# Dilated gated convolution on one core: load order, weight sums and first tiles by piece, last tiles transposed on TensorE, output-projection passes merged

## The chip, the cores and the metric

The kernel runs on one core of one Trainium2 chip. TensorE does the matrix products and transposes, VectorE and ScalarE the elementwise work, GpSimd some setup; a DMA is a copy between memories, issued from the queue of ScalarE, GpSimd or SyncE (SP). A semaphore is a counter that a finished step raises and a waiting one reads. The metric is the device time of one execution in microseconds (us). Before the change it is 387.62 us, the median of the three runs made before the prediction (386.77 to 388.38). Each run has its mean granted TensorE clock, as a share of full speed (0.971 in the profiled run of before).

## The reference, cut to what matters

```python
B, T, D, K = 2, 16000, 144, 15          # x: (B,T,D)  w: (K,D,2D)  w_o: (D,D), all bf16
dil = 2; pad = (K - 1) * dil            # 28
xp = pad x at the front by 28
h = sum over i of  xp[:, pad - 2*i : pad - 2*i + T, :] @ w[i]      # (B,T,288)
f, g = h[..., :144], h[..., 144:]
out = (tanh(f) * sigmoid(g)) @ w_o
```

The sequence is cut into 128 stretches of 250 steps, one per partition. A "tile" is one step of all 128 stretches, and an "oct" is 8 tiles. The 144 input channels are split into 128 (buffers with an A) and 16 (with a B, eight steps packed into one 128-row tile). The kernel saves multiplications: it works with sums of weights (WC, WS, WB[2]) and differences of tiles (VE, VF, DU, DE, DF, BE, BF). So VectorE has to prepare weight sums and tile differences before TensorE can begin its steady loop.

## The kernel before: the parts that matter

The kernel records operations with what they read and write. A list scheduler then fixes an order for each engine, and semaphores are planned from that order. The order is fixed when the program is built, so an instruction that waits holds everything behind it on its engine (in the trace of after, two weight loads on ScalarE's queue stand 4.72 us, and ScalarE's first copy comes behind them).

```python
# weights: three pieces on ScalarE's queue, three completion semaphores ("wa": 3 at the end)
wa_pieces = [(0, 5), (5, 10), (10, 15)]
for pi, (t0, t1) in enumerate(wa_pieces):
    g.add("act", ld_w(t0, t1), w=[("WA", pi)], dma="wa", ...)
...                                     # then the two WB loads, also on ScalarE's queue
# ScalarE: copies of the first x tiles (XBc, XA), then halving of the gate half of each piece
    g.add("act", lambda a: a.activation(WA[:, a_:b_, D:N2], ..., scale=0.5), w=[("WA", pi)])
# x: chunks of 32 steps in a ring of three, all queued at once on the other queue (SP)
XCH = 32
# weight sums: whole-array sums, after all pieces
wsum(WC[:, 1], WA[0,4,8,12], WA[2,6,10,14]);  wsum(WC[:, 2, 0:3], ...);  wsum(WC[:, 0], ...)
wsum(WS[:, 0:7], WA[even], WA[odd])
# out-projection weights, scaled by 0.5 on GpSimd
g.add("pool", lambda p: p.tensor_scalar(WOR[:], WOR[:], 0.5, None, ALU.mult), ...)

# a completion semaphore is taken from a small pool; a DMA that takes one again
# first waits for the DMA that had it before
def assign(self, mksem, dma_sems):
    ...
            slot = pool.pop(0); pool.append(slot)
            if slot[2] is not None:
                op.deps.add(slot[2])
    ...
g.assign(mksem, {"xp": 8, "wa": 3, "wb": 2, "xr": NX, "xa": 4, ...})

# out-projection of one oct: DMA transpose of Z, then two matmuls of 144 columns per tile
def ship(o):
    g.add("sp", lambda e: e.dma_start_transpose(ZT[...], Z[...]), dma="zt", ...)
    for dl in range(a, c):
        for part in range(2):
            t.matmul(PS[:, cc:cc + D], lhsT=ZT[:, zt, dl + part, :], rhs=WOR[:, 2*dl + part, :])
    ...                                 # ScalarE copy to OS, store
```

Cut: the tile differences, the four-stage loop S1 to S4 over 62 half-octs, tanh and gate (`finish_pair`), and the launch.

## Time and profile before

| | before |
|---|---|
| median time, us | 387.62 |
| span of the profiled run, us | 385.4 |
| mean granted TensorE clock in it | 0.971 |
| TensorE without a gap from / to, us | 36.45 / 375.7 |
| last weight piece lands, us | 22.33 |
| start of the last convolution matmul to the end (the tail), us | 10.01 |

The first view is the strip of 40 equal slices on the page of before: a digit is the busy share in tenths, and PEclk is the granted clock.

```profile
PE   5156999999999999999999999999999999999992
PEclk9559999999999999999999999999999999999997
```

TensorE is full from the fifth slice to the last but one. What can be gained lies at both ends.

The second view is the chain of waits of before, at the head: start, duration, what it was.

```profile
2.75 19.58 DMA WA<-in_w_dram
...
22.35 0.81 ACT WA L441
...
23.19 5.93 DVE WC L450 x2
...
29.14 0.62 DVE WC L450
...
36.02 0.38 DVE DD L646
...
36.45 2.87 PE PS L553 x22
```

The weights land at 22.33 us. Two sums then take 5.93 us together, while the next sum takes 0.62. The reason shows in GpSimd's timeline of before: its scaling of the out-projection weights ran at the same time.

```profile
22.37 6.04 POOL L724 TENSOR_SCALAR WOR<-WOR 128x2304 bf16<-128x2304 bf16 x1 [6.29 <-DMA WOR<-in_w_o_dram]
```

The third view is the same chain at the tail, after the last convolution matmul.

```profile
375.75 0.66 ACT TS L582
...
376.43 0.47 DVE Z L586
...
376.92 3.23 DMA ZT<-Z
...
380.20 2.20 PE PS L610 x16
```

The DMA transpose costs 3.23 us, and the sixteen matmuls behind it run at 0.138 us each; the same matmuls take 0.0625 us in the loop. The granted clock is 1.00 in the loop, 0.76 from 379 to 381 us and 0.50 after that.

### The profile page before, as it was taken

The numbers are of one execution on the slowest core, as the hardware profiler recorded it, in microseconds if no ns is written. First come the engines' busy times: TensorE is split into PE (matmuls) and PEld (weight loads), VectorE is DVE, ScalarE is ACT, GpSimd is POOL, SyncE is SP. The second block draws the span as 40 slices with busy tenths as digits, with TensorE's granted clock in tenths as the row PEclk, the third lists the DMA queues.
The fourth block names the chain that finished last, engine by engine and source line by source line (L and its number), as shares of the span: only waits on it lengthen the run. The fifth ranks groups of instructions, "written<-read, shape, count | busy, mean of one in ns | idle before, by whom it ended". The sixth has DMA issues, their size and how long they took to land.

```text
span 385.4 us, 7697 instructions
## 1 busy us (share of the span) xinstructions
PE 358.0 (93%) x3154; PEld 290.6 (75%) x3154; DVE 244.7 (63%) x629; ACT 173.1 (45%) x355; POOL 21.0 (5%) x31
## 2 busy tenths in 40 slices
PE   5156999999999999999999999999999999999992
PEld 5035888888888888888888888888888888888871
DVE  1759998766666757766666677666666665544340
ACT  2312453545445544454455444544544445444442
POOL 8660000000000000000000000000000000000000
PEclk9559999999999999999999999999999999999997
DMA  8972979785547457565437444654356433211222
GB/s 229 381 146 45 248 139 243 148 220 118 101 111 212 78 116 112 124 180 118 88 92 115 90 101 101 117 115 88 91 116 87 101 78 90 64 40 54 63 51 72
DMA packets 111599, 47.03 MB, mean 122 GB/s; under 512 B 103678, under 2 KB 106159, under 8 KB 110669
## 3 DMA queue, kind: packets, MB, share of 16 engines
q1 hardware_dynamic: 108826, 44.96, 52.7%
q10 hardware_dynamic: 2227, 1.25, 1.3%
q8 instruction: 24, 0.39, 0.4%
q0 software_dynamic: 512, 0.33, 0.3%
q14 instruction: 10, 0.08, 0.1%
HBM read 11.82 MB, written 9.22 MB: 55 GB/s over the span
## 4 chain that ended last, share of the span: by engine, by line
PE 89%; DMA 6%; DVE 3%; ACT 1%; ACTq 0%; issue 0%
PE PS L553 80%; PE PS L610 8%; DMA WA<-in_w_dram 5%; DVE WC L450 2%; DMA ZT<-Z 1%; DVE WS L450 0%; ACTq L342 0%; DVE Z L586 0%; ACT WA L441 0%; DVE STA L470 0%; DVE DU L499 0%; DVE VE L499 0%; DVE VF L499 0%; ACT TS L582 0%; ACTq L334 0%
## 5 line engine op out<-in xcount | busy, mean ns | idle before, releaser
L582 ACT ACTIVATE TS<-PS 128x576 bf16<-128x576 f32 x125 | 81.3, 650 | 100.8 <-PE PS L553 100.4
L586 DVE SCALAR_TENSOR_TENSOR Z<-TS 128x288 bf16<-128x288 bf16 x125 | 56.8, 455 | 42.3 <-ACT TS L582 42.0
L553 PE MATMUL PS<-WA,DE 128*128 128x288 bf16 x496 | 81.0, 286 | 0.0
L553 PE MATMUL PS<-WS,DU 128*128 128x288 bf16 x434 | 71.0, 286 | 2.1 <-DVE DD L646 2.1
L553 PE MATMUL PS<-WA,DF 128*128 128x288 bf16 x434 | 71.0, 286 | 0.0
L643 ACT ACTIVATE U<-PS 128x288 f32<-128x288 f32 x62 | 25.4, 410 | 71.1 <-PE PS L553 71.0
L553 PEld LDWEIGHTS PS<-WA,DE 128*128 128x128 bf16 x496 | 47.8, 98 | 11.2
L553 PEld LDWEIGHTS PS<-WS,DU 128*128 128x128 bf16 x434 | 42.3, 98 | 12.9 <-DVE DD L646 2.4
L615 ACT ACTIVATE OS<-PS 128x432 bf16<-128x432 f32 (+1 forms) x94 | 42.7, 487 | 20.4 <-PE PS L610 20.4
L553 PEld LDWEIGHTS PS<-WA,DF 128*128 128x128 bf16 x434 | 42.2, 98 | 10.3
L646 DVE TENSOR_TENSOR DD<-PS,U 128x288 f32<-128x288 f32 x62 | 28.3, 457 | 30.2 <-PE PS L553 19.7
L610 PE MATMUL PS<-WOR,ZT 128*128 128x144 bf16 x500 | 42.4, 229 | 4.5 <-DMA ZT<-Z 4.5
L610 PEld LDWEIGHTS PS<-WOR,ZT 128*128 128x128 bf16 x500 | 35.9, 99 | 8.4 <-DMA ZT<-Z 4.8
L553 PE MATMUL PS<-WC,VE 128*128 128x288 bf16 x248 | 40.5, 286 | 0.9 <-DVE VE L499 0.9
L553 PE MATMUL PS<-WC,XA 128*128 128x288 bf16 x248 | 40.5, 286 | 0.0
L499 DVE TENSOR_TENSOR BF<-XB 128x512 bf16<-128x512 bf16 x31 | 13.1, 423 | 37.5 <-PE PS L553 37.5
L553 PE MATMUL PS<-WB,XB 128*128 128x288 bf16 x128 | 36.6, 289 | 0.0
L553 PE MATMUL PS<-WB,BE 128*128 128x288 bf16 x124 | 35.5, 286 | 0.0
L553 PE MATMUL PS<-WB,BF 128*128 128x288 bf16 x124 | 35.5, 286 | 0.0
L553 PE MATMUL PS<-WC,VF 128*128 128x288 bf16 x186 | 32.9, 286 | 0.0
L660 DVE TENSOR_TENSOR PS<-PS,DD 128x288 f32<-128x288 f32 x62 | 28.6, 462 | 5.6 <-PE PS L553 0.9
L657 DVE TENSOR_TENSOR PS<-PS,DD 128x288 f32<-128x288 f32 x62 | 28.7, 462 | 0.8 <-PE PS L553 0.7
(61 smaller groups left out, 350.8 us busy)
## 6 DMA issues: line engine op xcount, KB each, us to landing
out_dram<-OS SPq DMA_DIRECT2D x31, 288.0 KB, 2.1
Xr<-in_x_dram SPq DMA_DIRECT2D x7, 1152.0 KB, 6.6
WA<-in_w_dram ACTq DMA_DIRECT2D x3, 360.0 KB, 14.3
Xr<-in_x_dram SPq DMA_DIRECT2D x1, 864.0 KB, 4.5
ZT<-Z SPq DMA_TRANSPOSE x32, 3.3
Xp<-in_x_dram SPq DMA_DIRECT2D x2, 252.0 KB, 5.5
XA<-STA SPq DMA_TRANSPOSE x31, 3.2
XB<-STB SPq DMA_TRANSPOSE x31, 3.2
```

The source lines that it names most:

```text
L450: g.add(eng, lambda v: v.tensor_tensor(dst(), a(), b(), ALU.add), r=r, w=wk, dur=dur)
L499: return g.add("dve", lambda v: v.tensor_tensor(dst(), a(), b(), ALU.subtract), r=r, w=wk, dur=dur)
L553: return lambda t: t.matmul(bank(b), lhsT=lhs(), rhs=rhs(), start=start, stop=True, skip_group_check=True)
L582: return a.activation(TS[:, s, :, :], src, ACT.Tanh)
L586: return v.scalar_tensor_tensor(dst, TS[:, s, :, D:N2], 1.0, TS[:, s, :, 0:D], ALU.add, ALU.mult)
L610: return t.matmul(PS[:, cc_:cc_ + D], lhsT=ZT[:, zt, dl_ + part_, :], rhs=WOR[:, 2 * dl_ + part_, :], start=first, stop=True, skip_group_c ...
L615: return a_.activation(OS[:, os_, a0:c0, :].rearrange("p e d -> p (e d)"), PS[:, bo * 512:bo * 512 + (c0 - a0) * D], ACT.Copy)
L643: g.add("act", lambda e: e.activation(U[:, u, :], bank(a), ACT.Copy), r=[("bank", a)], w=[("U", u)], dur=0.43)
L646: g.add("dve", lambda v: v.tensor_tensor(DD[:, u, :], bank(b), U[:, u, :], ALU.subtract), r=[("bank", b), ("U", u)], w=[("DD", u)], dur=0.48)
L657: g.add("dve", lambda v: v.tensor_tensor(bank(c), bank(a), DD[:, u, :], ALU.add), r=[("bank", a), ("DD", u)], w=[("bank", c)], dur=0.48)
L660: g.add("dve", lambda v: v.tensor_tensor(bank(e), bank(b), DD[:, u, :], ALU.subtract), r=[("bank", b), ("DD", u)], w=[("bank", e)], dur=0.48)
```

## The change

The intent:

1. Queue the x chunks, all but the first 8 steps, behind the last weight piece. Make the first chunks smaller (8, 8, 16, then 32).
2. Cut the weights into four pieces, and form weight sums and the first two ("direct") tiles piece by piece.
3. Delete the scaling on GpSimd. The factor 0.5 goes into an existing ScalarE copy.
4. Merge neighbouring out-projection matmuls that share a transposed block: 11 instead of 16 per oct, with the same columns in all.
5. In the last oct, transpose Z on TensorE instead of by DMA, two tiles at a time.

```diff
-        wa_pieces = [(0, 5), (5, 10), (10, 15)]
+        wa_pieces = [(0, 4), (4, 8), (8, 12), (12, 15)]
...
+    CH = [(0, 8), (8, 16), (16, 32)] + [(c, min(c + XCH, 8 * NOCT)) for c in range(32, 8 * NOCT, XCH)]
+        load_xchunk(1).deps.add(wa_op)            # likewise for all later chunks
...
-        g.add("pool", lambda p: p.tensor_scalar(WOR[:], WOR[:], 0.5, None, ALU.mult), ...)
+                    return a_.activation(OS..., PS..., ACT.Copy, scale=0.5)
...
-        wsum(lambda: WC[:, 1, :, :], lambda: wev(0, 4), lambda: wev(2, 4), wak, [("WC", 1)], 0.7)
+        for i in range(4):                        # sums of piece i as soon as it is there
+                wsum(lambda i=i: WC[:, 1:3, i, :], ..., [("WA", i)], [("WC", 1, i), ("WC", 2, i)], 0.4)
...
+                for blk in range(a, c + 1):       # one matmul of 144 or 288 columns per block
+                        return t.matmul(PS[:, c0:c0 + n * D], lhsT=ZT[:, zt, blk_, :], rhs=WOR[:, wi_:wi_ + n, :]...)
...
+        def ship_pair(o, dl, step, pb):           # last oct only, four times
+            for i in range(2):
+                t.transpose(PSb[:, ...128 columns], Z[:, z, c:c + 128], ID[:])
+                t.transpose(PSb[0:DB, ...128 columns], Z[:, z, c + 128:c + D], ID[:])       # DB = 16
+            ...                                   # VectorE and ScalarE copy to ZTL
+                t.matmul(PS..., lhsT=ZTL[:, q, 128 columns], rhs=WOR[:, 0, :])
+                t.matmul(PS..., lhsT=ZTL[0:DB, q, 128 columns], rhs=WOR[0:DB, 1, :])
```

Two smaller things of the diff are not in this list: the loads of the out-projection weights also wait for the last weight piece, and 16 throw-away matmuls stand behind each of the three pieces of the first x tiles, meant to keep TensorE warm (its granted clock high).

More of the change, by code (lines that the diff above doesn't have):

```diff
@@ L343, in ld_w @@
             return f
-        wa_pieces = [(0, 5), (5, 10), (10, 15)]
+        wa_pieces = [(0, 4), (4, 8), (8, 12), (12, 15)]
         for pi, (t0, t1) in enumerate(wa_pieces):
-            g.add("act", ld_w(t0, t1), w=[("WA", pi)], dur=0.55, dma="wa", nbytes=(t1 - t0) * 128 * N2 * 2)
+            wa_op = g.add("act", ld_w(t0, t1), w=[("WA", pi)], dur=0.55, dma="wa", nbytes=(t1 - t0) * 128 * N2 * 2)
         def ld_wb(par):
@@ L373, in cmp_op, with warm @@
             return g.add(eng, f, r=keys_r, w=[tag], dur=dur)
-        NWARM = 40
-        g.add("pe", [lambda t: t.matmul(PS[:, BANK_O * 512:BANK_O * 512 + 128], lhsT=ID[:], rhs=ONES[:], start=True, stop=True)] * NWARM,
-              r=["ID", "ONES"], w=[("bank", BANK_O)], dur=4.5)
-        cmp_tags = []
+        def warm(n):
+            g.add("pe", [lambda t: t.matmul(PS[:, BANK_O * 512:BANK_O * 512 + 128], lhsT=ID[:], rhs=ONES[:], start=True, stop=True)] * n,
+                  r=["ID", "ONES"], w=[("bank", BANK_O)], dur=0.07 * n)
+        warm(40)
         def compact_pro(pi):
@@ L411, in _conv_wavenet_kernel @@
             compact_pro(pi)
+            warm(16)
         for o in range(-4, 0):
@@ L443, in _conv_wavenet_kernel @@
         g.add("act", lambda a: a.activation(WB[:, 0:2, D:N2], WB[:, 0:2, D:N2], ACT.Copy, scale=0.5), w=[("WB", 0), ("WB", 1)], dur=0.45)
-        wak = [("WA", i) for i in range(3)]
+        wak = [("WA", i) for i in range(4)]
         def wev(t, n):
@@ L450, in wsum, with chunk_of @@
             g.add(eng, lambda v: v.tensor_tensor(dst(), a(), b(), ALU.add), r=r, w=wk, dur=dur)
+        def chunk_of(t):
+            return [ci for ci, (a, c) in enumerate(CH) if a <= t < c][0]
         def load_xchunk(ci):
-            e0 = E0 + XCH * ci
-            e1 = min(NE_ALL, e0 + XCH)
+            a, c = CH[ci]
             s = ci % NX
-            g.add("sp", ld_x(flat(Xr[:, s, 0:e1 - e0, :]), 0, NP, e0, e1), w=[("Xr", s)], dur=0.5, dma="xr", nbytes=NP * (e1 - e0) * D * 2)
+            return g.add("sp", ld_x(flat(Xr[:, s, 0:c - a, :]), 0, NP, E0 + a, E0 + c), w=[("Xr", s)], dur=0.5, dma="xr", nbytes=NP * (c - a) * D * 2)
         def compact_chunk(ci):
-            e0 = E0 + XCH * ci
-            e1 = min(NE_ALL, e0 + XCH)
+            a, c = CH[ci]
             s = ci % NX
-            n = e1 - e0
-            n4 = (n // 4) * 4
-            cmp_op("dve", Xr[:, s, 0:n4, DA:D], e0, e0 + n4, [("Xr", s)], ("XBc", ci), 0.06 + n4 * DB / 1900.0 + 0.1)
+            cmp_op("dve", Xr[:, s, 0:c - a, DA:D], E0 + a, E0 + c, [("Xr", s)], ("XBc", ci), 0.16 + (c - a) * DB / 1900.0)
         def load_xa(o):
             s, q = aslot(o), o % NST
-            ci, i0 = (8 * o) // XCH, (8 * o) % XCH
+            ci = chunk_of(8 * o)
+            i0 = 8 * o - CH[ci][0]
             g.add("dve", lambda v: v.tensor_copy(STA[:, q, :, :], Xr[:, ci % NX, i0:i0 + 8, 0:DA]),
@@ L480, in load_xb @@
                 if e >= E0:
-                    ck.add(("XBc", (e - E0) // XCH))
+                    ck.add(("XBc", chunk_of(e - E0)))
                 else:
@@ L592, in _conv_wavenet_kernel @@
         o_n = [0]
+        wor_keys = [("WORp", dl, part) for dl in range(8) for part in range(2)]
+        ZTL = sb("ZTL", [NP, 4, 512], BF16)
+        tl_n = [0]
+        last_store = {}
+        def ship_pair(o, dl, step, pb):
+            z, q = o % NZ, tl_n[0] % 4
+            os_ = (o + 1) % NO
+            tl_n[0] += 1
+            fns = []
+            for i in range(2):
+                c0 = (dl + i * step) * D
+                fns.append(lambda t, c=c0, i_=i: t.transpose(PSb[:, pb * 1024 + 128 * i_:pb * 1024 + 128 * i_ + 128], Z[:, z, c:c + 128], ID[:]))
+                fns.append(lambda t, c=c0, i_=i: t.transpose(PSb[0:DB, pb * 1024 + 1024 + 128 * i_:pb * 1024 + 1152 + 128 * i_], Z[:, z, c + 128:c + D], ID[:]))
+            g.add("pe", fns, r=[("Z", z, dl), "ID"], w=[("bank", pb), ("bank", pb + 1)], dur=0.3, floating=True)
+            g.add("dve", lambda v: v.tensor_copy(ZTL[:, q, 0:256], PSb[:, pb * 1024:pb * 1024 + 256]), r=[("bank", pb)], w=[("ZTL", q, 0)], dur=0.33)
+            g.add("act", lambda a: a.activation(ZTL[0:DB, q, 256:512], PSb[0:DB, pb * 1024 + 1024:pb * 1024 + 1280], ACT.Copy), r=[("bank", pb + 1)], w=[("ZTL", q, 1)], dur=0.38)
+            bo = BANK_O + o_n[0] % 2
+            o_n[0] += 1
+            fns = []
+            for i in range(2):
+                c0 = bo * 512 + i * D
+                fns.append(lambda t, c=c0, i_=i: t.matmul(PS[:, c:c + D], lhsT=ZTL[:, q, 128 * i_:128 * i_ + 128], rhs=WOR[:, 0, :],
+                                                          start=(i_ == 0), stop=True, skip_group_check=True))
+                fns.append(lambda t, c=c0, i_=i: t.matmul(PS[:, c:c + D], lhsT=ZTL[0:DB, q, 256 + 128 * i_:384 + 128 * i_], rhs=WOR[0:DB, 1, :],
+                                                          start=False, stop=True, skip_group_check=True))
+            g.add("pe", fns, r=[("ZTL", q, 0), ("ZTL", q, 1)] + wor_keys, w=[("bank", bo)], dur=0.3, floating=True)
+            op = g.add("act", lambda a: a.activation(bass.AP(OS[:].tensor, (os_ * 8 + dl) * D, [[NO * 8 * D, NP], [step * D, 2], [1, D]]),
+                                                PS[:, bo * 512:bo * 512 + 2 * D].rearrange("p (a b) -> p a b", a=2), ACT.Copy, scale=0.5),
+                  r=[("bank", bo)], w=[("OS", os_, dl)], dur=0.43)
+            op.deps.add(last_store[os_])
@@ L594, in ship, with store_some, f @@
+        def store_some(o, dls, step, n):
+            os_ = (o + 1) % NO
+            def f(e):
+                src = bass.AP(OS[:].tensor, (os_ * 8 + dls[0]) * D, [[NO * 8 * D, NP], [step * D, n], [1, D]])
+                dst = bass.AP(out_t, (KD + 8 * o + dls[0]) * D, [[L * D, NP], [step * D, n], [1, D]])
+                return e.dma_start(dst, src)
+            g.add("sp", f, r=[("OS", os_, d) for d in dls], w=[], dur=0.5, dma="st", nbytes=NP * n * D * 2)
         def ship(o):
@@ L605, in ship, with f @@
                 o_n[0] += 1
-                for dl in range(a, c):
-                    cc = bo * 512 + (dl - a) * D
-                    for part in range(2):
-                        def f(t, dl_=dl, cc_=cc, part_=part, first=(dl == a and part == 0)):
-                            return t.matmul(PS[:, cc_:cc_ + D], lhsT=ZT[:, zt, dl_ + part_, :], rhs=WOR[:, 2 * dl_ + part_, :],
-                                            start=first, stop=True, skip_group_check=True)
-                        fns.append(f)
-                g.add("pe", fns, r=[("ZT", zt), "WOR"], w=[("bank", bo)], dur=0.125 * (c - a), floating=True)
+                for blk in range(a, c + 1):
+                    q0, q1 = max(blk - 1, a), min(blk, c - 1)
+                    wi = 2 * blk - 1 if q0 == blk - 1 else 2 * blk
+                    def f(t, c0=bo * 512 + (q0 - a) * D, n=q1 - q0 + 1, blk_=blk, wi_=wi, first=(blk == a)):
+                        return t.matmul(PS[:, c0:c0 + n * D], lhsT=ZT[:, zt, blk_, :], rhs=WOR[:, wi_:wi_ + n, :].rearrange("p a b -> p (a b)"),
+                                        start=first, stop=True, skip_group_check=True)
+                    fns.append(f)
+                g.add("pe", fns, r=[("ZT", zt)] + wor_keys, w=[("bank", bo)], dur=0.11 * (c - a) + 0.06, floating=True)
                 def ev(a_, a0=a, c0=c, bo=bo):
                     return a_.activation(OS[:, os_, a0:c0, :].rearrange("p e d -> p (e d)"),
-                                         PS[:, bo * 512:bo * 512 + (c0 - a0) * D], ACT.Copy)
+                                         PS[:, bo * 512:bo * 512 + (c0 - a0) * D], ACT.Copy, scale=0.5)
                 g.add("act", ev, r=[("bank", bo)], w=[("OS", os_, a)], dur=0.19 + (c - a) * D / 1200.0)
@@ L621, in stf @@
                 return e.dma_start(dst, OS[:, os_, d0:8, :].rearrange("p e d -> p (e d)"))
-            g.add("sp", stf, r=[("OS", os_, a) for a, _ in groups], w=[], dur=0.5, dma="st", nbytes=NP * (8 - d0) * D * 2)
+            last_store[os_] = g.add("sp", stf, r=[("OS", os_, a) for a, _ in groups], w=[], dur=0.5, dma="st", nbytes=NP * (8 - d0) * D * 2)
         quads = [(o, r) for o in range(NOCT) for r in range(2)]
@@ L631, in S1 @@
             g.add("pe", region(a, [(lambda o_=o - i: XA[:, aslot(o_), r, :]) for i in range(4)], [wc(0, i) for i in range(4)], True),
-                  r=[("XA", aslot(o - i)) for i in range(4)] + [("WC", 0)], w=[("bank", a)], dur=4 * MM)
+                  r=[("XA", aslot(o - i)) for i in range(4)] + [("WC", 0, i) for i in range(4)], w=[("bank", a)], dur=4 * MM)
             g.add("act", lambda e: e.activation(bank(b), bank(a), ACT.Copy), r=[("bank", a)], w=[("bank", b)], dur=0.43)
@@ L639, in S2 @@
             g.add("pe", region(a, [(lambda o_=o - i: VE[:, vslot(o_), r, :]) for i in range(4)], [wc(1, i) for i in range(4)]),
-                  r=[("VE", vslot(o - i)) for i in range(4)] + [("WC", 1)], w=[("bank", a)], dur=4 * MM)
+                  r=[("VE", vslot(o - i)) for i in range(4)] + [("WC", 1, i) for i in range(4)], w=[("bank", a)], dur=4 * MM)
             u = u_n[0] % NU
@@ L644, in S2 @@
             g.add("pe", region(b, [(lambda o_=o - i: VF[:, vslot(o_), r, :]) for i in range(4)], [fc(i) for i in range(4)]),
-                  r=[("VF", vslot(o - i)) for i in range(4)] + [("WC", 2), ("WA", 2)], w=[("bank", b)], dur=4 * MM)
+                  r=[("VF", vslot(o - i)) for i in range(4)] + [("WC", 2, i) for i in range(3)] + [("WA", 3)], w=[("bank", b)], dur=4 * MM)
             g.add("dve", lambda v: v.tensor_tensor(DD[:, u, :], bank(b), U[:, u, :], ALU.subtract), r=[("bank", b), ("U", u)], w=[("DD", u)], dur=0.48)
@@ L651, in S3 @@
             a, b, u = QB[n]
-            kd = [("DU", vslot(o - i)) for i in range(4)] + [("WS",), ("WA", 2)] + xbk(o) + [("WB", 2)]
+            kd = [("DU", vslot(o - i)) for i in range(4)] + [("WS", i) for i in range(4)] + [("WA", 3)] + xbk(o) + [("WB", 2)]
             g.add("pe", region(a, [(lambda o_=o - i: DU[:, vslot(o_), r, :]) for i in range(4)] + [lambda: XB[:, bslot(o), 4 + r, :]],
@@ L680, in S4, with direct @@
             give(e)
-            if r == 1:
-                ship(o)
-        def direct(k, b):
-            e = H + k
-            keys = [("XA", aslot(o)) for o in range(-4, 0)] + wak + [("XB", bslot(-1)), ("WB", 0), ("WB", 1)]
-            tiles = [(lambda e_=e - DIL * i: xa_tile(e_)) for i in range(K)] + [lambda: xb_tile(e), lambda: xb_tile(e - 2)]
-            ws = [(lambda i_=i: WA[:, i_, :]) for i in range(K)] + [lambda: WB[:, 0, :], lambda: WB[:, 1, :]]
-            g.add("pe", region(b, tiles, ws, True), r=keys, w=[("bank", b)], dur=17 * MM)
+            if o == NOCT - 1:
+                ship_pair(o, r, 6, b if r else BANK_O)
+                ship_pair(o, 2 + r, 2, e if r else BANK_O)
+                if r == 0:
+                    store_some(o, [0, 2], 2, 4)
+                else:
+                    store_some(o, [1], 6, 2)
+                    store_some(o, [3], 2, 2)
+            elif r == 1:
+                ship(o)
+        def direct(bb):
+            xa4 = [("XA", aslot(o)) for o in range(-4, 0)]
+            for pi, (t0, t1) in enumerate(wa_pieces):
+                for k in range(KD):
+                    e = H + k
+                    g.add("pe", region(bb + k, [(lambda e_=e - DIL * i: xa_tile(e_)) for i in range(t0, t1)], [(lambda i_=i: WA[:, i_, :]) for i in range(t0, t1)], pi == 0),
+                          r=xa4 + [("WA", pi)], w=[("bank", bb + k)], dur=(t1 - t0) * MM)
+            for k in range(KD):
+                e = H + k
+                g.add("pe", region(bb + k, [(lambda e_=e: xb_tile(e_)), (lambda e_=e: xb_tile(e_ - 2))], [lambda: WB[:, 0, :], lambda: WB[:, 1, :]]),
+                      r=[("XB", bslot(-1)), ("WB", 0), ("WB", 1)], w=[("bank", bb + k)], dur=2 * MM)
         load_xchunk(0)
+        load_xchunk(1).deps.add(wa_op)
+        for o in range(-4, 0):
+            v_first(o)
         load_xa(0)
@@ L696, in _conv_wavenet_kernel @@
         load_xb(0)
-        load_xa(1)
-        direct(0, 4)
-        direct(1, 5)
-        wsum(lambda: WC[:, 1, :, :], lambda: wev(0, 4), lambda: wev(2, 4), wak, [("WC", 1)], 0.7)
-        wsum(lambda: WC[:, 2, 0:3, :], lambda: wev(1, 3), lambda: wev(3, 3), wak, [("WC", 2)], 0.55)
-        wsum(lambda: WC[:, 0, 0:3, :], lambda: WC[:, 1, 0:3, :], lambda: WC[:, 2, 0:3, :], [("WC", 1), ("WC", 2)], [("WC", 0)], 0.55)
-        wsum(lambda: WC[:, 0, 3, :], lambda: WC[:, 1, 3, :], lambda: WA[:, 13, :], [("WC", 1)] + wak, [("WC", 0)], 0.22)
-        for o in range(-4, 1):
-            v_first(o)
-        wsum(lambda: WS[:, 0:7, :], lambda: bass.AP(WA[:].tensor, 0, [[16 * N2, NP], [2 * N2, 7], [1, N2]]),
-             lambda: bass.AP(WA[:].tensor, N2, [[16 * N2, NP], [2 * N2, 7], [1, N2]]), wak, [("WS",)], 1.1)
-        wsum(lambda: WB[:, 2, :], lambda: WB[:, 0, :], lambda: WB[:, 1, :], [("WB", 0), ("WB", 1)], [("WB", 2)], 0.22)
+        direct(4)
+        for i in range(4):
+            if i < 3:
+                wsum(lambda i=i: WC[:, 1:3, i, :], lambda i=i: WA[:, 4 * i:4 * i + 2, :], lambda i=i: WA[:, 4 * i + 2:4 * i + 4, :], [("WA", i)], [("WC", 1, i), ("WC", 2, i)], 0.4)
+                wsum(lambda i=i: WC[:, 0, i, :], lambda i=i: WC[:, 1, i, :], lambda i=i: WC[:, 2, i, :], [("WC", 1, i), ("WC", 2, i)], [("WC", 0, i)], 0.25)
+            else:
+                wsum(lambda: WC[:, 1, 3, :], lambda: WA[:, 12, :], lambda: WA[:, 14, :], [("WA", 3)], [("WC", 1, 3)], 0.25)
+                wsum(lambda: WC[:, 0, 3, :], lambda: WC[:, 1, 3, :], lambda: WA[:, 13, :], [("WC", 1, 3), ("WA", 3)], [("WC", 0, 3)], 0.25)
+        v_first(0)
         for o in range(-3, 1):
             v_second(o)
+        for i in range(4):
+            n = 2 if i < 3 else 1
+            wsum(lambda i=i, n=n: WS[:, 2 * i:2 * i + n, :], lambda i=i, n=n: bass.AP(WA[:].tensor, 4 * i * N2, [[16 * N2, NP], [2 * N2, n], [1, N2]]),
+                 lambda i=i, n=n: bass.AP(WA[:].tensor, (4 * i + 1) * N2, [[16 * N2, NP], [2 * N2, n], [1, N2]]), [("WA", i)], [("WS", i)], 0.4 if n == 2 else 0.25)
+        wsum(lambda: WB[:, 2, :], lambda: WB[:, 0, :], lambda: WB[:, 1, :], [("WB", 0), ("WB", 1)], [("WB", 2)], 0.25)
         for o in range(-3, 1):
@@ L722, in f @@
                     return e.dma_start(WOR[r0_:r1_, i_, :], bass.AP(wo_t, s0_ * D, [[D, r1_ - r0_], [1, D]]))
-                g.add("pool", f, r=["WORz"], w=[("WORp", dl, part)], dur=0.5, dma="wor", nbytes=(r1 - r0) * D * 2)
-        g.add("pool", lambda p: p.tensor_scalar(WOR[:], WOR[:], 0.5, None, ALU.mult), r=["WORz"] + [("WORp", dl, part) for dl in range(8) for part in range(2)],
-              w=["WOR"], dur=2.5)
+                op = g.add("pool", f, r=["WORz"], w=[("WORp", dl, part)], dur=0.5, dma="wor", nbytes=(r1 - r0) * D * 2)
+                op.deps.add(wa_op)
+        load_xa(1)
         ship(-1)
         NQ = len(quads)
-        chunks_loaded = 1
+        chunks_loaded = 2
         chunks_done = 1
@@ L735, in prep @@
             nonlocal chunks_done
-            while chunks_done * XCH < 8 * (o + 1):
+            while chunks_done < len(CH) and CH[chunks_done][0] < 8 * (o + 1):
                 compact_chunk(chunks_done)
@@ L746, in fetch @@
             nonlocal chunks_loaded
-            while chunks_loaded * XCH < min(8 * (o + 4), 8 * NOCT):
-                load_xchunk(chunks_loaded)
+            while chunks_loaded < len(CH) and CH[chunks_loaded][0] < 8 * (o + 4):
+                load_xchunk(chunks_loaded).deps.add(wa_op)
                 chunks_loaded += 1
```

## The prediction

> **What bounds the kernel now.** Of the 385.4 us span, TensorE streams without a gap from 36.45 to 375.7 us (timeline and engine windows: PE busy throughout, clock 1.00). That middle, 339.3 us, is all column time: 2,521 matmuls of 288 columns at about 122.5 ns (the chain of waits has 74 in 9.06 us) and 484 out-projection matmuls of 144 columns at 62.5 ns (12 in 0.75 us). So the change can gain at the two ends, 36.45 us of head and 9.7 us of tail, and hardly in the middle.
>
> **Head, before.** Chain of waits: third weight piece landing at 22.33 us, its halving on ScalarE 0.81, two weight sums on VectorE 5.93, smaller sums to 31.6, then thirteen VectorE operations to the first gapless matmul at 36.45. Two things are avoidable.
> - The weight pieces wait behind x: 360 KB took from about 8 to 16.5, and again to 22.3 us (50-60 GB/s) while all queues moved 376-400 GB/s. [...] The change defers all x but 8 rows until the weights have landed: I estimate 14-16 us.
> - The first big weight sum took 5.4 us while GpSimd scaled the out-projection weights (22.37 to 28.4 us); the 864-column sum right after took 0.61, so the pair should cost about 1.45. [...] The change deletes the GpSimd scaling (the 0.5 goes into an existing ScalarE copy).
>
> After: VectorE limits the head. From about 11.6 us (first weights halved) it has some 6 us of sums, copies and compactions, then thirteen tile differences at 0.335 = 4.4 us, a gate, a copy and a subtraction: first gapless matmul at 23-24 us, 12-13 earlier. The direct tiles in pieces should keep TensorE warm. But XA and XB of the second oct are now loaded after the weights and transposed at 22-28 us, just in time instead of 10 us early; transposes take 3.2 us to land, and VectorE was already 92% busy in 36-50 us. I charge 1-3 us of new TensorE gaps in the first two octs. Head net: -11 us.
>
> **Middle.** Merging turns 16 matmuls per oct into 11 with the same columns. Only the roughly 2.5 ns fixed part of 151 matmuls goes: 0.4 us.
>
> **Tail.** Before: last convolution matmul 375.73, tanh 0.66, gate 0.47, DMA transpose 3.23, 16 cold matmuls 2.2, copy 0.4, store to 385.4. After, four TensorE transposes, a VectorE and a ScalarE copy (about 0.4 each step) and four matmuls replace the DMA transpose. But ScalarE and VectorE handle four pairs one after another, so about 6.3 us remain, and 0.25-0.5 us of transposes and stalls enter the stream before. Net: -3 us.
>
> **Prediction: 373 us** (387.6 - 11 - 0.4 - 3), 80% range 368.5 to 378. Faster by over 2%: 0.95; within 2%: 0.04; slower by over 2%: 0.01.
>
> **What would show it.** Weights landing by 16 us; no sum over 1 us; gapless TensorE from 23-26 us; small waits for VE, DD or XA in 23-40 us; a middle of the same length; 6-7 us from last convolution matmul to end.
>
> **What would make it wrong.** Weights after 18 us [...]; second-oct tiles several us late, since every wait in the fixed order delays all engines; TensorE cold at the loop's start (up to 2 us); the last oct's transposes stalling TensorE behind a busy ScalarE, eating the tail's gain.

(Three passages are cut where marked, because no run here shows what they say: why the weight pieces lose to x on the queues, by what means GpSimd's scaling slows VectorE's sum, and a guess about the weight rows. No term of the sum is cut: 387.6 - 11 - 0.4 - 3 is 373.2, put on record as 373. The 2.5 ns in the middle is an estimate from the two step times that the prediction gives: 2 x 62.5 - 122.5. The 14 to 16 us for the weights and the "up to 2 us" for a cold TensorE were estimates, without a sum beside them; measured were 11.60 us and some 1.7 us. That the pieces of direct tiles "should keep TensorE warm" was expected, not shown.)

(Two figures of it are rough. 360 KB in the 8.8 us to 16.47 and the 5.9 us to 22.33 us are 42 and 63 GB/s. Its tail of 9.7 us is counted from the end of the last convolution matmul, 0.3 us less than in the tables here.)

## The result and the profile after

| | before | after |
|---|---|---|
| median time, us (runs of the same rounds) | 387.53 (4 runs) | 378.19 (4 runs, 377.69 to 379.57) |
| ratio, 95% interval | | 0.976 (0.973 to 0.980) |
| span of the profiled run, us | 385.44 | 377.85 |
| mean granted clock in it | 0.971 | 0.987 |
| last weight piece lands, us | 22.33 | 11.60 |
| first loop matmul behind the head's long wait, us | 36.45 | 26.11 |
| start of the 41st matmul of the loop's first stage, us | 83.81 | 76.91 |
| start of the last convolution matmul to the end (the tail), us | 10.01 | 9.05 |

A ratio here is the mean time of one kernel's fast runs over that of the other's of the same rounds, so it is not quite the ratio of the medians. The change is faster by 2.4%. The predicted 373.0 us was 5.2 us too low, and the result lies just outside the range.

The gain in the two profiled spans is 7.6 us. At the 41st matmul of the loop's first stage, where both kernels run undisturbed, after is 6.9 us ahead. The tail is 0.96 us shorter. The stretch between is 0.27 us longer: the merge shortens it, but the first TensorE transposes now lie in it (c1_unmerged and c1_tail_dma below give the two parts). (The medians differ by 9.3 us; the profiled run of after was its slowest.)

The strip of after:

```profile
PE   8668999999999999999999999999999999999996
PEclk9999999999999999999999999999999999999996
```

The chain of waits of after, at the head, answers to the one above:

```profile
1.72 5.35 DMA WA<-in_w_dram
7.09 0.38 ACTq L343
7.50 0.72 ACTq L353
8.26 0.84 ACTq L353
9.62 1.01 ACT XA L410
10.86 0.43 DVE VE L501
...
25.68 0.38 DVE DD L689
26.11 5.78 PE PS L555 x32
```

No long sum is left. But the chain begins with the landing of the first weight piece, at 7.07 us. What that landing releases is not a use of the weights: it is the issue of another load (L343, the weights), then the issue of the two WB loads (L353), and only then ScalarE's first copies. ScalarE's timeline of after shows it from the other side; ACTq is the issue of DMAs on ScalarE.

```profile
2.75 4.72 ACTq L343 DMA_DIRECT2D WA<-in_w_dram  x2
7.50 1.60 ACTq L353 DMA_DIRECT2D WB<-in_w_dram  x2
9.23 0.23 ACT L389 ACTIVATE XBc<-Xp 128x32 bf16<-128x32 bf16 x1 [6.33 <-issue]
```

And VectorE's timeline of after has the consequence, a gap of 2.99 us before 10.75 us:

```profile
10.75 0.07 DVE L419 MEMSET XA<- 128x16 bf16 x1 [2.99 <-ACT XA L410]
```

The view of what TensorE waited for in after has as its longest wait, once the loop has begun:

```profile
PE PS L555 <- DVE DD L689: 2.4, 1, 2.4
```

In the table of engines by stretch of after (length, busy times, then granted clock, DMA share and GB/s), TensorE stands still from 24 to 26 us and then gets 0.59 of its clock:

```profile
24.00:26.00 2.00, 0.00 (x0) 0.00 (x0) 2.00 (x6) 0.00 (x0) 0.00 (x0) 1.00 0.79 304
26.00:30.00 4.00, 3.89 (x19) 2.56 (x20) 2.83 (x9) 0.41 (x1) 0.00 (x0) 0.59 0.67 129
```

The tail of after, in the chain of waits:

```profile
370.31 0.42 ACT OS L623
...
370.78 0.23 PE PS L608
371.01 0.15 PE PS L609
...
374.85 0.24 PE PS L620
...
375.11 0.41 ACT OS L623
```

Transposes (L608, L609) and small matmuls (L618, L620) follow each other every 0.15 to 0.18 us at full clock and about every 0.23 us at the lower clock that follows (granted 0.62 from 371 to 373 us and 0.50 from 373 to 375 us). There are 32 of them, and from 370.78 to 375.09 us the chain consists of nothing else.

The low clock is a matter of the run. The same instructions in the trace of p2_wa4 (the first experiment below; its tail is the one of after) kept a granted clock of 1.00 until 369.2 us, and steps of 0.15 to 0.18 us up to the last one at 369.37 us. In its chain of waits:

```profile
366.44 0.15 PE PS L609
...
369.04 0.16 PE PS L620
```

There the tail takes 8.13 us, and 8.07 in x1_filler, instead of 9.05. So some 0.9 us of the tail in the trace of after is the clock, and not the steps.

### The profile page after: what moved, and what is told of

It is laid out like the page before. It is cut to its first block, busy times and chain, and to the rows that moved or that the text cites. A ratio compares the mean times of both kernels' runs of the same rounds, so it can differ in the third digit from the quotient of the medians.

```text
span 377.9 us, 7552 instructions
## 1 busy us (share of the span) xinstructions
PE 364.5 (96%) x3067; PEld 290.3 (77%) x3067; DVE 242.2 (64%) x642; ACT 174.2 (46%) x361; POOL 15.0 (4%) x30
## 4 chain that ended last, share of the span: by engine, by line
PE 91%; DVE 5%; DMA 1%; ACT 1%; ACTq 1%; issue 0%
PE PS L555 81%; PE PS L653 8%; DMA WA<-in_w_dram 1%; DVE WC L452 1%; DVE VE L501 1%; PE PS L618 0%; PE PS L620 0%; DVE VF L501 0%; DVE DU L501 0%; DVE DE L501 0%; ACTq L353 0%; DVE STA L472 0%; PE PS L609 0%; DVE WS L452 0%; PE PS L608 0%
## 5 line engine op out<-in xcount | busy, mean ns | idle before, releaser
L658 ACT ACTIVATE OS<-PS 128x432 bf16<-128x432 f32 (+1 forms) x91 | 41.2, 488 | 13.9 <-PE PS L653 13.6
L653 PE MATMUL PS<-WOR,ZT 128*128 128x144 bf16 (+1 forms) x333 | 39.8, 253 | 0.0
L653 PEld LDWEIGHTS PS<-WOR,ZT 128*128 128x128 bf16 x333 | 27.8, 98 | 5.8
L703 DVE TENSOR_TENSOR PS<-PS,DD 128x288 f32<-128x288 f32 x62 | 28.6, 462 | 5.2 <-PE PS L555 0.9
L555 PEld LDWEIGHTS PS<-WC,VE 128*128 128x128 bf16 x248 | 24.1, 98 | 7.3 <-ACT PS L676 0.8
```

The lines of the kernel that those rows point to most:

```text
L555: return lambda t: t.matmul(bank(b), lhsT=lhs(), rhs=rhs(), start=start, stop=True, skip_group_check=True)
L653: return t.matmul(PS[:, c0:c0 + n * D], lhsT=ZT[:, zt, blk_, :], rhs=WOR[:, wi_:wi_ + n, :].rearrange("p a b -> p (a b)"), start=first, st ...
L658: return a_.activation(OS[:, os_, a0:c0, :].rearrange("p e d -> p (e d)"), PS[:, bo * 512:bo * 512 + (c0 - a0) * D], ACT.Copy, scale=0.5)
L703: g.add("dve", lambda v: v.tensor_tensor(bank(e), bank(b), DD[:, u, :], ALU.subtract), r=[("bank", b), ("DD", u)], w=[("bank", e)], dur=0.48)
```

## The experiments

Two theories for the missing 5 us:

- **H (head):** the fourth load takes the first load's semaphore again, so it stands on ScalarE's queue until the first has landed, at 7.07 us, and everything behind it waits (the first copy, at 9.23 us, comes after 6.33 us that the trace puts down to issue). ScalarE's copies, and with them all of VectorE's chain, start late for that.
- **T (tail):** the pieces of 16 rows or 16 columns make each transpose and matmul slow. The number of steps in the tail is not what costs.
- **Rivals:** VectorE's amount of work sets the head, so an earlier start only moves the wait; and in the tail, the four copies one after another on ScalarE set the length whatever TensorE does.

Except where an edit is itself a reordering, made by hand after scheduling, all the variants keep the order of the other instructions on every engine. (In c1_tail_dma and c3_order_bank the last oct is planned anew.) Two marks are used below: **the gate matmul**, the one behind the wait for DD (26.11 us in after), and **the settled mark**, the start of the 41st matmul of the loop's first stage (76.91 us in after).

### p2_wa4: a semaphore for each weight load

```diff
-        g.assign(mksem, {"xp": 8, "wa": 3, ...
+        g.assign(mksem, {"xp": 8, "wa": 4, ...
```

> The changed kernel with four completion semaphores for the weight loads instead of three, one per piece; the order of every engine is the same. Theory (new wait made by the change): the fourth weight load can be issued only when the first has landed, at 7.07 us, and ScalarE's copies stand behind it; freed, ScalarE's first copy starts about 1 us earlier than 9.23, VectorE's long busy stretch starts before 10 instead of 10.75, and the first matmul after the wait comes at about 25.3 instead of 26.1; time down by 0.5 to 1 us. Rival: ScalarE's queue is held anyway by the issuing of the loads behind it (in the kernel before it issued until 8.4 us with no such wait), so ScalarE starts at 8.5 to 9 and the time changes by less than 0.4 us.

Measured: 375.46 us (374.1 to 376.37), ratio to before 0.968 (0.966 to 0.971). That is 2.7 us less than after. ScalarE's timeline of this run:

```profile
2.75 1.12 ACTq L343 DMA_DIRECT2D WA<-in_w_dram  x2
3.91 2.37 ACTq L353 DMA_DIRECT2D WB<-in_w_dram  x2
6.41 0.23 ACT L389 ACTIVATE XBc<-Xp 128x32 bf16<-128x32 bf16 x1 [3.50 <-POOL WOR L361]
```

The first copy starts at 6.41 instead of 9.23 us, the gate matmul at 23.20 instead of 26.11. The last weights landed at 11.55 against 11.60 us, so this is not about the weights. I had expected only 0.5 to 1 us. The direction was right and the size far too small: the whole 2.9 us is passed on to the gate matmul. (The profiled run of p2 was its fastest, and its trace has no cold stretch from 20 to 50 us: the granted clock is 1.00 there.)

### x3_full_width: the tail with full blocks

Each tile's second block is now its own columns 16 to 144 instead of 128 to 144, against a zero-padded copy of the weights. All blocks are 128x128, and the result is the same. (ScalarE's copy takes 128 rows instead of 16, and one more small load fills slot 16.)

```diff
-  t.transpose(PSb[0:DB, ...], Z[:, z, c + 128:c + D], ID[:])
+  t.transpose(PSb[:, ...],    Z[:, z, c + 16:c + 144], ID[:])
-  t.matmul(PS..., lhsT=ZTL[0:DB, ...], rhs=WOR[0:DB, 1, :])
+  t.matmul(PS..., lhsT=ZTL[:, ...],    rhs=WOR[:, 16, :])     # slot 16: rows 112..127 = w_o[128:144], else 0
```

> The changed kernel with the 16-column second block of each tile of the last oct replaced by a 128-column block of the same tile (columns 16 to 144, out-projected with weights that are zero but for the last 16 rows), so that all transposes and matmuls of the tail have full width; the order of every engine is the same. Theory (narrow blocks alternate with full ones and the weight load no longer overlaps): the 32 instructions of the tail come every 0.155 us warm and 0.23 us cold in the changed kernel; with full width they should come every 0.06 to 0.12 us, the stretch from the last convolution matmul to the end should fall from 8.8 to 6 to 7 us, and the time by 1.5 to 2.5 us. Rival (a chain through ScalarE and VectorE, bank waits, and a cold clock set the tail): it stays above 8 us, time within 0.6 us of 378.2.

Measured: 375.30 us (374.93 to 375.9), ratio 0.968 (0.965 to 0.971), 2.9 us less than after. The tail takes 6.49 us instead of 9.05. TensorE does more arithmetic and is faster. At equal clock the gain is smaller, for in p2_wa4 and x1_filler the narrow tail took 8.1 us: some 1.6 us of tail, and 0.40 in the stream before (291.49 us from the settled mark to the last convolution matmul, 291.89 in after). The rest of the 2.6 us is the low clock of after's tail. How the steps changed is shown for c1_both below.

### x1_filler: keep TensorE busy in the 2.4 us wait

```diff
+ 36 matmuls of 128 columns into an unused bank, right after the first part of S3(0)
```

> The changed kernel with 36 throw-away matmuls put into TensorE's 2.4 us wait before the second half of the first quad's third stage; no other instruction moves. Theory (cold clock): in the changed kernel that wait drops the granted clock to 0.59 in 26 to 30 us, and some 27 matmuls take about 0.2 to 0.24 us instead of 0.1225; with the filler the clock stays 1.00 there, and the time falls by 1 to 1.7 us, to about 376.5 to 377. Rival (VectorE's fixed order sets the pace there whatever TensorE's clock): the clock is repaired but new waits of the same length appear at 30 to 37 us, and the time stays within 0.4 us of 378.2.

Measured: 379.11 us (377.16 to 380.41), ratio 0.977: no gain. In the profiled run the clock was 1.00 in 26 to 30 us, and the settled mark came at 75.46 instead of 76.91 us. From the gate matmul to that mark it took 49.13 instead of 50.80 us, so there the cold stretch had cost some 1.7 us. (In after about 14 matmuls from 26.73 to 30.1 us take 0.24 us each; the 27 of the expectation are too many.) But that run, the fastest of the six, had a mean clock of 0.992, and the five others had 0.984 to 0.987; where they were cold, no trace tells. The profiled run too was cold elsewhere (0.64 in 14 to 16 us, 0.51 in 16 to 18; its mean clock of 0.992 over 375.4 us is some 3.0 us short of full speed, and none of that lies between 20 and 50 us). The experiment is inconclusive: warming this spot does not decide the clock of the run.

### x4_dd_early: the DD instruction eight places earlier on VectorE

```diff
+ dv = g.order["dve"]; i0 = dv.index(DD of the first half-oct)
+ dv.insert(i0 - 8, dv.pop(i0))
```

> The changed kernel with one VectorE instruction moved: the first quad's subtraction stands after 4 of the 8 second differences instead of behind all of them, two more, a gate and a copy; nothing else moves. Theory (order): TensorE's 2.4 us wait before the third stage's second half disappears (the next is a wait of about 1.2 us before the fourth stage), the clock stays at 1.00, and the time falls by 1.5 to 2.5 us. Rival (VectorE's total work until the second oct is what counts, in any order): the waits only move to 29 to 37 us and the time falls by less than 0.6 us.

Measured: 380.52 us (378.67 to 382.85), 2.3 us more than after. The wait for DD is gone, and this wait is new in the list of what TensorE waited for (another, for a sum on VectorE, took 1.0 us):

```profile
PE PS L555 <- DMA XA<-STA: 3.0, 1, 3.0
```

To move one instruction forward moved the wait to the next thing that was late, the transpose of the second oct's tile. The rival held for this edit, in that the wait moved; that the time would rise, neither side had said.

### c1_both: both repairs together

```diff
  # the edits of p2_wa4 and x3_full_width, applied to the changed kernel
```

> The changed kernel with both repairs that paid alone: a completion semaphore for each of the four weight loads (alone 375.5 us) and full-width blocks in the last oct (alone 375.3 us); the order of every engine is that of the changed kernel. If the two act in different stretches, as the traces say (head 2.9 us earlier, tail 2.6 us shorter), the gains add: 372.5 us, between 372 and 373.3. Rival [...]: 374 or more.

Measured: 373.55 us (372.05 to 374.1), ratio 0.962 (0.959 to 0.965). The prediction for the change had been 373.0. (What the rival was is cut from the recorded text, because no run here shows it; its figure, 374 or more, stands.) The two gains add to 4.6 us of the 5.6 that they gave one by one. (The difference fits the clock: with a narrow tail at full clock, full blocks gain some 2.0 us, not 2.9.) The tail takes 6.54 us, and one pair of it looks like this in the chain of waits of this run:

```profile
367.15 0.23 PE PS L608
367.38 0.06 PE PS L609
...
367.58 0.39 ACT ZTL L612
...
368.02 0.24 PE PS L618
```

At full clock in both (granted 1.00 in c1_both from 363 to 369 us, and in after from 367 to 371), a step of the same kind now takes 0.06 us where it took 0.15 us, and the chain runs through ScalarE's copies (0.39 to 0.42 us each), as the prediction had it. The timelines of weight loads (PEld) and matmuls (PE) show a difference beside it. In after, at full clock:

```profile
367.68 0.22 PE L608 MATMUL PS<-ID,Z 128*128 128x128 bf16 x1
367.83 0.22 PE L609 MATMUL PS<-ID,Z 128*16 128x128 bf16 x1
367.83 0.09 PEld L609 LDWEIGHTS PS<-ID,Z 128*16 128x16 bf16 x1 [0.17 <-issue]
```

And in x3_full_width, where these instructions are as in c1_both:

```profile
366.73 0.22 PE L608 MATMUL PS<-ID,Z 128*128 128x128 bf16 x1
366.78 0.22 PE L609 MATMUL PS<-ID,Z 128*128 128x128 bf16 x1
366.73 0.10 PEld L609 LDWEIGHTS PS<-ID,Z 128*128 128x128 bf16 x1
```

With full blocks, the load for the second transpose starts together with the first transpose, 0.05 us ahead of its own. With alternating sizes it starts only with its own, 0.15 us after the first. So in these records the load no longer starts beside the matmul before it. That the size is the cause is shown by x3 and the full-clock tails above (0.06 us a step against 0.15 to 0.18); why TensorE does so is not.

The six runs fall in two groups: clock 0.994 or 0.995 with 373.82 to 374.1 us, and clock 0.999 or 1.0 with 372.05 to 373.27 us. The profiled run is of the first group, with a cold stretch at 24 to 26 us. One such stretch, some 3.4 us at half clock in the records (granted 0.91 in 22 to 24 us, 0.50 in 24 to 26 and 0.87 in 26 to 30; in after 0.50 from 26.7 to 30.1), is worth some 1.7 us here (50.81 us from the gate matmul to the settled mark, 49.14 in p2_wa4's trace without one). What starts and ends it, and why some runs of the same program have it and others not, is not shown.

### c1_unmerged: c1_both with 16 matmuls per oct again

```diff
-                for blk in range(a, c + 1):       # 144 or 288 columns
+                for dl in range(a, c):
+                    for part in range(2):         # 144 columns each, as before the change
```

> The version with both repairs, with the out-projection passes of two tiles not merged: 16 matmuls of 144 columns per oct again, all else the same. By the prediction's term the merge is worth 0.4 us: time up by 0.4, and the stretch from the third oct to the last convolution matmul (291.9 us) longer by 0.4. Rival (that stretch was 291.6 us in the kernel before, unmerged, so the merge saves nothing there): no change within 0.3 us, the stretch equal or shorter.

Measured: 374.39 us (372.52 to 374.75), ratio 0.964 (0.961 to 0.967). The intervals overlap, so the time alone does not decide. The profiles do: from the settled mark to the last convolution matmul it is 291.82 us unmerged and 291.49 us merged, 0.34 us for the merge. An estimate from the trace of before: two steps of 144 columns take 2 x 62.5 ns there and one of 288 takes 122.5, so a matmul saved is worth about 2.5 ns; the 135 fewer in this stretch (of 151 in all) make 0.34 us, as measured.

### c1_tail_dma: c1_both with the DMA transpose in the last oct

```diff
-            if o == NOCT - 1:
+            if False:
                 ship_pair(...)
```

> The version with both repairs, with the last oct sent through the DMA transpose as in the kernel before; nothing before the last oct moves. Theory: from the last convolution matmul to the end 10.0 us again instead of 6.5, and the time up by 3 to 3.5 us. Rival (transposes and bank waits inside the stream give back most of it): up by less than 2 us.

Measured: 375.85 us (375.27 to 377.15). The tail is 9.99 us again. The stretch before is 0.22 us shorter, because no transposes lie in it. By these stretches the TensorE transposes with full blocks gain 3.2 us, which is in the expected range. The medians differ by only 2.3 us, but they mix runs of two clocks: this version has four runs at 0.990 or 0.991 (375.27 to 375.95 us) and two at 0.986 (376.85 to 377.15), and these groups lie each 3 us above those of c1_both. By the same stretches the narrow blocks of the change gain 0.3 us in the trace of after (9.05 us of tail, and 0.63 more in the stream) and 1.2 where the clock stayed full (8.13).

### p1_no_pool_scale: before, with only the GpSimd scaling removed

```diff
-        g.add("pool", lambda p: p.tensor_scalar(WOR[:], WOR[:], 0.5, None, ALU.mult), ...)
-    a_.activation(OS..., PS..., ACT.Copy)
+    a_.activation(OS..., PS..., ACT.Copy, scale=0.5)
```

> The kernel before with one thing of the change alone: the halving of the out-projection weights on GpSimd is gone, and the 0.5 is applied by the existing ScalarE copies; no other instruction moves. Theory (the big weight sum is slow because GpSimd works at the same time): the two weight sums take about 1.45 us together instead of 5.93, the first gapless matmul comes at 32 instead of 36.45 us, and the time falls by 4 to 4.6 us, to about 383. Rival (the sum is slow for its own size, or the chain is held by something else at 24 to 29 us): the sums stay above 4 us, or the time falls by less than 2 us.

Measured: 384.55 us (383.91 to 385.7) against 387.41, ratio 0.991 (0.988 to 0.993). VectorE's timeline has the same two sums, which took 5.92 us beside the scaling:

```profile
23.70 1.28 DVE L450 TENSOR_TENSOR WC<-WA 128x1152 bf16<-128x1152 bf16 x2 [5.32 <-ACT WA L441]
```

This confirms that the scaling made the sums slow: they take 4.6 us less with nothing else changed. By what means one engine slows the other is not shown. Only 2.9 us reached the end, though. The weights landed 0.5 us later in this run, and the first loop matmul came only 2.3 us earlier: TensorE still did its direct tiles late (from 24.05 us) and cold (granted clock 0.50 in 24 to 26 us, 0.68 in 26 to 30), and VectorE's gating instruction for them (Z), which holds what stands behind it, now waited 1.10 us.

### c1_nodefer: c1_both with the x chunks not deferred

The second and third x chunks go right behind the first on their queue, without waiting for the weights.

```diff
+ for k in (1, 2):
+     xr[k].deps.discard(wa_op); move xr[k] behind xr[k - 1] in SP's order
```

> The version with both repairs, with the x loads of the second to fourth 8-row blocks (0.9 MB) issued at once behind the first instead of after the weights have landed; nothing else moves. Theory A (arrival of the weights is what the head gained from): the last weight piece lands 2 us or more after 11.6 us and the first matmul after the long wait comes 1 us or more later. Theory B (VectorE's chain has been the limit since about 8 us, and the weights are there 3 to 5 us before their sums' turn): the last piece lands at 13 to 15 us and neither that matmul nor the time moves by more than 0.5 us; the earlier x does not help either, since its copies stand behind the same chain.

Measured: 375.09 us (371.93 to 376.39), ratio 0.966 (0.962 to 0.969), 1.5 us more than c1_both. The last weights landed at 15.43 instead of 12.29 us, and the gate matmul came 2.2 us later. That fits the theory that the weights' arrival rules. But ScalarE's timeline has something else as well:

```profile
4.28 4.50 ACTq L353 DMA_DIRECT2D WB<-in_w_dram  x2
8.91 0.23 ACT L389 ACTIVATE XBc<-Xp 128x32 bf16<-128x32 bf16 x1 [5.99 <-issue]
```

The issue of the two WB loads held ScalarE for 4.50 us; in c1_both it was 2.46. Its first copy came at 8.91 instead of 6.50 us, which is 2.4 us late, about as much as the gate matmul. So there was a rival, B': the issue, not the arrival. (One of the six runs, at clock 1.0, took 371.93 us, as little as any of c1_both; only one run has a trace.)

### c1_nodefer_wbsp: the same, with the two WB loads on the other queue

```diff
+ for op in the two WB loads: move it from ScalarE's order to SP's, behind the x chunks
```

> The version with both repairs and x not deferred (375.1 us, against 373.6 with x deferred), with the two small weight loads issued from the sync engine's queue behind the x loads instead of from ScalarE's. In the run without this, ScalarE was held for 4.5 us in issuing them and started its copies at 8.9 instead of 6.5 us. Theory B' (what the deferral buys is ScalarE's freedom, not the weights' arrival): ScalarE starts by 6.5 us although the last weight piece still lands at 14 to 16 us, the first matmul after the long wait comes at about 23.5 instead of 25.7, and the time is back at 373 to 374. Theory A (arrival of the weights): that matmul stays at 25 us or later, time 374.8 or more.

Measured: 379.17 us (378.15 to 380.26). ScalarE starts at 5.27 us, and VectorE's first copy of the x chunk at 12.24, close to the 12.00 of c1_both, although the last weights land at 13.87. But the WB loads now stood behind x in their queue and came so late that TensorE waited for them:

```profile
PE PS L555 <- ACT WB L445: 8.2, 1, 8.2
```

As a test by time it failed: it made a new and larger wait.

### d1_nodefer_wblate and its control d3_both_wblate

Both move the two WB loads behind ScalarE's first three copies, on the same queue; d1 without the deferral of x, d3 (and c1_both) with it.

```diff
+ wb = the two WB loads; remove them from ScalarE's order
+ ac[k0 + 3:k0 + 3] = wb
```

> c1_nodefer (the x chunks not deferred) with the two WB loads moved in ScalarE's order behind its first three copies. Theory B' (without the deferral ScalarE was only held 2.4 us longer while it issued the two WB loads, and all later work started late for that): ScalarE's first copy starts at 6.5 us or earlier although the last weights still land at 13.5-15.5 us, the half-gap matmul S3b(0) starts at 23-24 us, as with the deferral (23.5), and the time is 373-374 us. Theory A (the weights' arrival itself decides): the first copy is early too, but S3b(0) stays at 25 us or later and the time at 374.7-375.5 us.

> c1_both (x deferred) with the same move of the two WB loads, as a control for the move alone. ScalarE's first copy at 4.5-5.5 us instead of 6.5; if VectorE's chain is then bound by the x pieces and the weights, S3b(0) moves by less than 0.5 us and the time stays at 373-374 us; if ScalarE's early start still counts, S3b(0) comes 1 us earlier and the time is near 372.5 us.

Measured: d1 372.32 us (371.75 to 374.22), ratio 0.960 (0.957 to 0.963); d3 373.69 us (371.84 to 374.05), ratio 0.961 (0.958 to 0.964). ScalarE's timeline of d1:

```profile
5.26 0.23 ACT L389 ACTIVATE XBc<-Xp 128x32 bf16<-128x32 bf16 x1 [2.35 <-DMA Xp<-in_x_dram]
6.67 1.60 ACTq L353 DMA_DIRECT2D WB<-in_w_dram  x2
15.38 0.56 ACT L443 ACTIVATE WA<-WA 128x432 bf16<-128x432 bf16 x1 [1.03 <-DMA WA<-in_w_dram]
```

The weights land as late as in c1_nodefer (15.35 us), and yet the gate matmul is at 23.24 us; in d3, with the weights at 11.96 us, it is at 23.30. So B' holds: in the repaired kernel the last weights may come at 15 us for nothing, because VectorE gets to their sums later. The medians of d1 and d3 differ by which clock a run happened to get. At clock 1.0 d1 ran in 371.75 to 372.49 us (four runs) and d3 in 371.84 to 372.15 (two); at 0.994 or 0.995, 373.8 to 374.22 (two) and 373.6 to 374.05 (four). The deferral of two x chunks is worth nothing that these runs can see. (All these kernels have the smaller x chunks, which put only 32 steps of x ahead of the weights; what the chunk sizes alone give was not tried.)

Why the issue of the same two loads takes 2.4 us in one run and 4.5 in another, the traces do not say: the semaphore that the second one waits for was set before 2 us.

### c2_order: VectorE's head in another order

39 VectorE instructions between the first tile differences and the third DD were reordered by hand, and two transposes swapped. Nothing was added or removed.

```diff
+ dv[35:74] = [dv[i] for i in [35, 36, 37, 48, 38, 39, 40, 49, 50, 41, 42, 43, 51, 44, 45, 53, 46, 47, 54, 55,
+                              56, 63, 64, 65, 52, 57, 58, 59, 60, 69, 72, 67, 68, 70, 71, 73, 61, 62, 66]]
+ sp[13:16] = [sp[13], sp[15], sp[14]]     # DD of the first three half-octs: old places 50, 56 and 73
```

> The version with both repairs (373.6 us) with 39 VectorE instructions and 2 transposes of the first two octs in another fixed order, by hand: what releases TensorE (the subtractions, the sums into PSUM) and what starts a transpose (the copy for the second oct's tiles) as soon as its inputs are there, second differences in between. Theory (what is left of the head's waits is the order, not the amount of VectorE's work): the 2.4 us wait and the 0.8 us one go, no new wait over 0.8 us comes before 40 us, the first matmul of the third oct comes at 37 to 38 instead of 39.2 to 41.2 us, time 370.5 to 372. Rival (amount): waits of the same sum appear later, as when one subtraction alone was moved, time 373 or more.

Measured: 371.26 us (370.17 to 371.88), ratio to before 0.956 (0.953 to 0.959). With d2_order_wblate below, which is the same within the noise, it is the fastest version here, 2.3 us better than c1_both, and beats both the kernel before and the change. The gate matmul is at 21.37 us, and the longest single wait left in the loop's beginning is 1.1 us, for a tile difference (BE); 0.8 had been expected at most. All six runs have a clock of 0.997 or more, so part of the 2.3 us is the cold stretch that half the runs of c1_both had, by their clock; against the others of c1_both it is about 1.3 us.

The amount of VectorE work is unchanged, so what was left in c1_both was its order. x4 and c2 together teach how such an order is changed: one instruction moved alone made it worse, a whole stretch ordered by need made it better.

### c3_order_bank: c2_order with another bank in the tail

A bank is a part of the memory that TensorE writes its results to.

```diff
-                ship_pair(o, 2 + r, 2, e if r else BANK_O)
+                ship_pair(o, 2 + r, 2, e)
```

> As the reordered version, and in the last oct the second tile pair is transposed into a free bank pair of its own, so that its transposes do not wait for the first pair's output copy (a wait of 0.57 us in the full-width run); the planner then also places the last oct's instructions otherwise. Theory (bank wait is on the tail's chain): tail 5.8 to 6 us instead of 6.5, time 0.5 lower than the reordered version. Rival (another chain through ScalarE, which in this plan does two output copies before the last tanh): tail 6.5 us or more.

Measured: 371.41 us (370.91 to 372.24). The tail shrank from 6.56 to 5.74 us, but the stretch before grew by 1.0 us, where TensorE now waits for ScalarE's copies inside the stream. What was gained was given back.

### d2_order_wblate: c2_order with the WB loads late

```diff
+ the edit of d3_both_wblate, on c2_order
```

> c2_order (hand order of VectorE's head) with the same move. Same question on the best version: S3b(0) within 0.5 us of 21.4 and 371.3 us, or 1 us earlier and near 370.3 us.

Measured: 371.16 us (369.52 to 371.46), ratio 0.955 (0.952 to 0.958). The gate matmul came 0.7 us earlier (20.70), the time did not move beyond the noise (medians 0.1 us apart).

## Why the prediction was right or wrong

**Right: the direction and what limits.** TensorE's middle did not move; the gain came from the ends. The long sums went away (no single one in after takes over 0.46 us). p1 shows that the GpSimd scaling was their cause. TensorE stayed warm in the head until the 2.4 us wait (granted 1.00 until 26.6 us; before was at half clock from 12 to 28 us). The weights landed early, even earlier (11.60 us) than the estimated 14 to 16.

**Right: the merge.** 0.4 us predicted, 0.34 measured in a stretch that holds 135 of the 151 matmuls.

**Wrong step 1: "first gapless matmul at 23-24 us ... Head net: -11 us".** Measured in after: the gate matmul at 26.11 us, and 6.9 us gained at the settled mark. The prediction counted VectorE's work from "about 11.6 us (first weights halved)" and took for granted that what VectorE needs from ScalarE before would be there. It was not: a fourth load on a pool of three semaphores held ScalarE until 9.2 us. p2 removes only that, and the gate matmul is at 23.20 us, in the predicted window, with the settled mark at 72.34 us, 11.5 earlier than before (in the profiled run, without a cold stretch). Four loads on a pool of three could be read in the program before the prediction; the wait was not costed.

**Mis-sized: "I charge 1-3 us of new TensorE gaps in the first two octs".** From the gate matmul to the settled mark it took 47.36 us in before and 50.80 in after, 3.4 us more. Some 1.7 us of these are the cold stretch after the 2.4 us wait (49.14 us in p2_wa4, which had none); the other 1.8 are within the charge. The prediction had named a cold TensorE among the things that could make it wrong, but had not charged it.

**Wrong step 2: the tail, "Net: -3 us".** The prediction wrote about 0.4 us for each step, 6.3 us left, and "0.25-0.5 us of transposes and stalls" in the stream. Measured in after: 9.05 us left (8.76 from the end of the last convolution matmul, as the prediction counts), so 1.0 gained, and 0.63 us in the stream. The steps that were mis-sized are the transposes and small matmuls: with blocks of 16 they follow each other every 0.15 to 0.18 us warm and 0.23 cold, and TensorE, not ScalarE, limits the tail. Of the 2.0 us missing in after's tail, 0.9 is the low clock of that run; at full clock the narrow tail is 8.1 us. With full blocks (x3, c1) the tail is 6.5 us (6.2 or 6.3 from that end), 0.22 us lies in the stream, and the chain is the predicted one.

**The two steps account for the miss.** With both repaired, the time is 373.55 us; predicted was 373.0. That it comes so close is in part luck: the six runs lie at 372.05 to 373.27 or at 373.82 to 374.1 us, by their clock.

**Right for an incomplete reason: the deferral.** The prediction made the weights' early arrival the core of the head's gain. In before it was (the chain of waits begins with it). In the changed kernel d1 shows that an arrival anywhere from 12 to 15 us gives the same time, once ScalarE is not held.

**Left open.** Where the other runs of x1 were cold; why the issue of the WB loads holds ScalarE for different times; what starts a cold stretch; by what means GpSimd's scaling slows VectorE's sums; what the small x chunks, the later out-projection weight loads and the added throw-away matmuls give alone.

## What to carry to other kernels

When a load is cut into more pieces, count the completion semaphores too: a DMA that waits for a recycled one stood here on a compute engine's queue and held that engine's other work (the two loads took 4.72 us in after, 1.12 with a semaphore each), which cost 2.7 us. When a transpose or matmul has a remainder of 16, try a full-size block with zeros: it was more arithmetic and here 2.9 us faster, some 2.0 of it at equal clock. When two traces are compared, compare the granted clock of the stretch first (here it was 0.9 us of 9.05 in the tail of after). And before costing an engine's work from the moment its last input arrives, check every other producer on its way, and in which order it gets there.
